# A gated linear attention feeding a mixture of four attention experts: three tile shapes on TensorE, and TensorE's order taken from a list scheduler in the source

## The chip, the core and the metric

One NeuronCore of one Trainium2 chip runs the whole program. The metric is device time in microseconds of one execution. A TensorE (PE) matmul names the part of the array that it uses: 128x128 (all of it), 64x128 (half of the rows), 128x64 or 128x32 (a half or a quarter of the columns). Matmuls on different parts of the array can run side by side.

## The reference

The first half is a gated linear attention over 4 batches, 8 heads, 768 steps, head size 48; its output is the input x of the second half, four causal attention experts of head size 64, of which each token takes two.

```python
for t in range(S):
    state = alpha[:, :, t, :, None] * state + np.einsum('bhd,bhe->bhde', k[:, :, t], v[:, :, t])
    y[:, :, t] = np.einsum('bhd,bhde->bhe', q[:, :, t], state)
...
logits = x @ w_gate                      # top 2 of 4, softmax over the two
for e in range(E):
    q = x @ wq[e]; k = x @ wk[e]; v = x @ wv[e]
    scores = scale * (q @ k.transpose(0, 2, 1))      # causal
    scores = scores - scores.max(-1, keepdims=True)
    a = np.exp(scores)
    a /= a.sum(-1, keepdims=True) + 1e-09
    ye = a @ v @ wo[e]
    out += mask[..., None] * w[:, :, kk:kk + 1] * ye
```

## The kernel before, in words

**The linear attention** goes in 24 chunks of 128 steps, 6 for each batch. For chunk n, `prep_r` and `prep_c` (L172, L185) make the decay products: two scans of 112x516 and one or two multiplies on VectorE (DVE), and from chunk 6 on one multiply on GpSimd (POOL). `gla_a` (L199) forms key times query for 8 heads in 64x128 tiles (`pa`); DVE masks one half into `ms`, ScalarE (ACT) copies and POOL masks the other. `gla_t` (L218) transposes the keys (`pt`, `kt`), `gla_u` (L228) updates the state with `pu`, in 128x64 tiles with 48 columns used, and `gla_y` (L252) makes the output `py` in 128x32 tiles, four abreast; ACT and DVE split it into `xh` and `xl`. `check` (L195) is one square on ACT that looks for lost precision.

**The experts** go in 8 units u of 384 tokens, three chunks each; two units make a batch, and an odd unit (hf = 1) sees twice the keys. `front(u)` has four projections `proj` (`pj`, 9 matmuls of 128x384 each), three value blocks `vproj` (`pv`, 9 of 128x260) and the gate. `back(u)` works on two pairs of experts: `top` (L471) finds each query's maximum over scores in 64x128 tiles (`sm`, reduced by DVE at L491 and L494), `toprow` transposes the three results (`pm`), and `score` (L507) forms the transposed scores (`sc`, 8 matmuls a step, two abreast; a step is one block of 128 keys), which ACT turns into exponentials `at` (L523), POOL masks on the diagonal (L525) and adds up into `as` (L533, L536). `av` (L538) multiplies them by the values (`yv`, two experts abreast in 128x64 tiles), and `sums` (L556) forms the denominators `ss` of one pair, two abreast in 128x32 tiles. `fin(u)` has `factor`, `scale` (transposes `pr`) and three `outp` (`po`, 6 matmuls of 128x384 each). There are 6 score steps in an even unit's back and 12 in an odd one's, 72 in all.

**Order.** PSUM has 8 banks, all under one tag. The head (chunks 0 to 2) and the body (unit 0's front, chunk 3's start) are in an order written by hand. From there Python generators are mixed: `mix` (L653) always advances the stream with the smallest cost divided by its weight, so `back(u)`, `front(u+1)` and the chunks of the half after next alternate with fixed weights (L44 to L52). What is emitted is then ordered on each engine by the framework's own scheduler. `AHEAD = 3` and `GROUP = 3` set how far `av` trails `score`. Loads are issued from ACT's queue in `gla` (L374), outputs from SyncE's (SP).

```python
b, g = back(0), half(1)
mix((b, MIX_BACK0), (g, MIX_GLA), until=g)
for u in range(NU - 2):
    mix((b, MIX_BACK[u]), (front(u + 1), MIX_FRONT[u]), (half(u + 2), 12.0))
    b = back(u + 1, fin(u))
```

Of the kernel before, what the change touches and what calls it, by code (L numbers as in the profile page):

```python
# [19 lines left out]
NE, HD = 4, 64  # L20
# [20 lines left out]
AHEAD = 3  # L41
GROUP = 3

HOP = 100  # L44
MIX_BACK0 = 6
MIX_BACK = (6, 22, 14, 22, 14, 22)
MIX_FRONT = (10, 10, 10, 10, 10, 10)
MIX_BACK6 = 10
MIX_TAIL6 = 20
MIX_TAIL7 = 28  # L50
MIX_FRONT7 = 12
MIX_GLA = 10  # L52
# [3 lines left out]
def tile_gla_moe(ctx: ExitStack, tc: tile.TileContext, qk_d, al_d, v_d, wqk_d, wv_d, wo_d, nat_d, vn_d, out_d):  # L56
# [142 lines left out]
    def gla_a(n):  # L199
        t = gl["qk", n]  # L200
        ms = work.tile([128, 2, 4, C], F32, name="ms", bufs=1)
# [16 lines left out]
    def gla_t(n):  # L218
# [5 lines left out]
        kt = gin.tile([128, 4, P], F32, name="kt")  # L224
# [3 lines left out]
    def gla_u(n):  # L228
# [50 lines left out]

    zb = d1r.rearrange("p a b -> p (a b)").bitcast(BF)[:, 0:256]  # L280
# [7 lines left out]
    cmask = consts.tile([128, 640], BF)  # L288
# [6 lines left out]
    def late_consts():  # L295
# [4 lines left out]
        A.activation(cmask[:, 512:640], sel, AF.Copy)  # L300
# [73 lines left out]
    def gla(h):  # L374
        for n in range(HALF * h, HALF * h + HALF):
            if n == HALF:
                prep_r(n + 1)
                yield
                prep_c(n + 1)
                yield  # L380
            if n + 2 < NG:
                load_v(n + 2, A)
            if n + 3 < NG:
                load_al(n + 3, 0, 4, A)
                load_q(n + 3, 0, 4, A)
            gla_y(n)
            gla_u(n)
            if n + 1 < NG:
                gla_a(n + 1)
                if (n + 1) % NC != NC - 1:  # L390
                    gla_t(n + 1)
            yield
            if n + 2 < NG:
                prep_r(n + 2)
                yield
                prep_c(n + 2)
                yield
                check(n + 1)
            yield


    mo = {}
    W3 = 384

    def proj(u, pair, which):
# [32 lines left out]
    def gate(u):  # L438
# [14 lines left out]
        w = work.tile([128, 3, NE], F32, name="gw")  # L453
# [17 lines left out]
    def top(u, pair, i):  # L471
        b, hf = divmod(u, 2)
        q, k = mo["q", u, pair], mo["k", b, pair]
# [4 lines left out]
        c1 = 384 if n == 640 else min(n, 512)  # L478
# [3 lines left out]
        for c0, c1 in pieces:  # L482
            w = c1 - c0
            pp = [gp("sm0"), gp("sm1")]
            for e in (0, 1):
                r = slice(64 * e, 64 * e + 64)
                mm(pp[e][:, :w], q[r, 0, 128 * i:128 * i + 128], k[r, 0, c0:c1], max(w, 256) / 4.8, start=True, stop=True,
                   tile_position=(64 * e, 0))
            for e in (0, 1):
                if c1 < n:  # L490
                    V.tensor_reduce(mp[:, e:e + 1], pp[e][:, :w], axis=AX.X, op=OP.max)  # L491
                else:
                    junk = work.tile([128, 512], BF, name="junk", bufs=2)
                    V.tensor_tensor_reduce(junk[:, :w], pp[e][:, :w], cmask[:, 640 - w:640], 1.0,  # L494
                                           -3.0e38 if c0 == 0 else mp[:, e:e + 1], OP.add, OP.max, mx[:, i, 64 * e:64 * e + 1])

    def toprow(u, pair):
# [5 lines left out]
        mr = work.tile([128, W3], F32R, name="mr", bufs=2)  # L503
# [3 lines left out]
    def score(u, pair, j):  # L507
        b, hf = divmod(u, 2)
        q, k, mr = mo["q", u, pair], mo["k", b, pair], mo["mr", u, pair]
# [4 lines left out]
        js = slice(128 * j, 128 * j + 128)  # L514
# [12 lines left out]
        if j == 1:  # L527
            s = work.tile([128, 2, W3], F32, name="as", bufs=2)
# [9 lines left out]
    def av(u, pair, j):  # L538
        b, hf = divmod(u, 2)
        at = mo.pop(("at", u, pair, j))  # L540
# [15 lines left out]
    def sums(u, pair):  # L556
        s = mo.pop(("as", u, pair))
        if pair == 0:
            mo["ss", u] = work.tile([128, W3], F32, name="ss", bufs=1)
        ss = mo["ss", u]  # L560
        ps_ = gp("ss")
        for e in (0, 1):
            r = 64 * pair + 32 * e
            mm(ps_[r:r + 32, :W3], ones32, s[:, e], W3 / 1.2, start=True, stop=True, tile_position=(0, r))
        r = slice(64 * pair, 64 * pair + 64)
        A.activation(ss[r], ps_[r, :W3], AF.Copy)
# [43 lines left out]

    def front(u):
# [10 lines left out]
    def fin(u):  # L622
        yield factor(u)
        for pair in (0, 1):
            yield scale(u, pair)
        for i in range(3):
            yield outp(u, i)

    def back(u, before=None):
        before = before or iter(())  # L630
        for pair in (0, 1):
            for i in range(3):
                yield top(u, pair, i)
            if pair == 0:
                yield next(before, None)
            yield toprow(u, pair)
        nj = 3 * (u % 2) + 3
        steps = [(pair, j) for pair in (0, 1) for j in range(nj)]
        for x in range(0, len(steps) + AHEAD, GROUP):
            for p, j in steps[x:x + GROUP]:  # L640
                yield score(u, p, j)
            yield next(before, None)
            for p, j in steps[max(0, x - AHEAD):max(0, x - AHEAD + GROUP)]:
                yield av(u, p, j)
                if j == nj - 1:
                    yield sums(u, p)
        yield from before

    def chain(*gs):
        for x in gs:  # L650
            yield from x

    def mix(*streams, until=None):  # L653
        live = [[g, w, 0.0] for g, w in streams if g is not None]
        while live and (until is None or any(x[0] is until for x in live)):
            x = min(live, key=lambda z: z[2] / z[1])
            c0 = cost[0]
# [158 lines left out]
```

## Time and profile before

| | |
|---|---|
| median of 3 runs | 434.1 us (432.31 to 435.65) |
| the profiled execution's own time | 432.75 us |
| its span, first to last instruction | 431.0 us |
| mean granted TensorE clock, share of 2.4 GHz | 0.924 |
| PE busy | 392.5 us, 91% |
| DVE, ACT, POOL busy | 255.9, 181.9, 183.8 us |

PE's busy time is made of modelled ends: a matmul counts from its start until its result is out, so matmuls in a stream overlap, and a short wait hides between two of them. What a matmul costs in a stream is therefore read from start to start. PEclk is the granted clock as a share of 2.4 GHz; 0.50 is 1.2 GHz.

### The profile page before, as it was taken

The numbers are of one execution on the slowest core, as the hardware profiler recorded it, in microseconds if no ns is written. First come the engines' busy times: TensorE is split into PE (matmuls) and PEld (weight loads), VectorE is DVE, ScalarE is ACT, GpSimd is POOL, SyncE is SP. The second block draws the span as 40 slices with busy tenths as digits, with TensorE's granted clock in tenths as the row PEclk, the third lists the DMA queues.
The fourth block names the chain that finished last, engine by engine and source line by source line (L and its number), as shares of the span: only waits on it lengthen the run. The fifth ranks groups of instructions, "written<-read, shape, count | busy, mean of one in ns | idle before, by whom it ended". The sixth has DMA issues, their size and how long they took to land.

```text
span 431.0 us, 9692 instructions
## 1 busy us (share of the span) xinstructions
PE 392.5 (91%) x3914; PEld 290.9 (67%) x3914; DVE 255.9 (59%) x615; ACT 181.9 (42%) x422; POOL 183.8 (43%) x234
## 2 busy tenths in 40 slices
PE   7989796998998799999998979999999999999953
PEld 5679475776676577777686756877677767646633
DVE  5979999899974537574955614472743324661120
ACT  1265352653263525534264344553244525335621
POOL 2122199543177560761249460370127433307520
PEclk9899776999699989999889969999979999999966
DMA  8936436454041422323222301201000010001101
GB/s 236 325 103 205 151 110 187 136 161 149 0 113 45 136 73 68 108 73 98 69 84 70 113 37 44 68 26 40 17 2 2 20 38 0 2 19 38 56 2 64
DMA packets 14022, 35.41 MB, mean 82 GB/s; under 512 B 1616, under 2 KB 5136, under 8 KB 13968
## 3 DMA queue, kind: packets, MB, share of 16 engines
q10 hardware_dynamic: 7600, 22.02, 16.8%
q1 hardware_dynamic: 6368, 12.68, 9.1%
q8 instruction: 33, 0.54, 0.6%
q14 instruction: 21, 0.17, 0.1%
HBM read 29.98 MB, written 4.72 MB: 80 GB/s over the span
## 4 chain that ended last, share of the span: by engine, by line
PE 53%; DVE 14%; POOL 9%; issue 8%; ACT 7%; DMA 6%; SPq 0%; ACTq 0%; POOLq 0%; DVEq 0%
PE pj L73 12%; PE sc L73 7%; PE yv L73 7%; PE po L73 7%; DMA al<-in_al_dram 5%; PE py L73 4%; PE pv L73 3%; DVE al L178 3%; PE sm L73 3%; PE pa L73 2%; PE ss L73 2%; ACT al L197 2%; POOL as L536 2%; DVE al L189 2%; POOL qk L183 2%
## 5 line engine op out<-in xcount | busy, mean ns | idle before, releaser
L536 POOL TENSOR_TENSOR as<-as,at 128x256 f32<-128x256 f32 (+2 forms) x40 | 56.2, 1404 | 13.9 <-DVE gmx L466 8.8
L523 ACT ACTIVATE at<-sc 128x384 f32<-128x384 f32 (+1 forms) x144 | 50.2, 425 | 12.4 <-PE sc L73 11.1
L73 PE MATMUL sc<-q,k 64*128 64x384 f32 (+2 forms) x432 | 53.1, 339 | 0.3 <-ACT at L523 0.3
L533 POOL TENSOR_TENSOR as<-at 128x512 f32<-128x512 f32 (+1 forms) x16 | 26.7, 1668 | 62.1 <-ACT at L523 61.5
L73 PE MATMUL yv<-at,vg 128*64 128x384 f32 (+2 forms) x288 | 46.5, 439 | 4.9 <-DVE xl L277 3.3
L178 DVE TENSOR_TENSOR_SCAN al<-al,d1r 112x516 f32<-112x516 f32 (+1 forms) x25 | 36.7, 1471 | 15.2 <-DMA al<-in_al_dram 15.2
L73 PEld LDWEIGHTS sc<-q,k 64*128 64x128 f32 x432 | 36.7, 191 | 13.3 <-issue 6.4
L250 POOL TENSOR_TENSOR S<-st,ev 48x192 f32<-48x192 f32 x32 | 20.6, 644 | 54.1 <-DVE st L249 53.1
L525 POOL TENSOR_SCALAR_AFFINE_SELECT at<-at 128x256 f32<-128x256 f32 x48 | 26.8, 558 | 35.4 <-ACT at L523 35.4
L73 PE MATMUL pj<-xh,wqk_h 128*128 128x384 f32 x96 | 38.8, 404 | 1.8 <-DVE xl L277 1.0
L494 DVE CUSTOM_DVE_ANT_0 junk<-sm,cmask 128x128 bf16<-128x128 f32 (+3 forms) x64 | 28.2, 481 | 19.1 <-PE sm L73 19.0
L73 PE MATMUL py<-ms,v 128*32 128x128 f32 x768 | 37.8, 287 | 1.2 <-DVE ms L212 0.9
L73 PE MATMUL sm<-k,q 64*128 64x256 f32 (+3 forms) x128 | 32.9, 431 | 5.1 <-DVE ms L212 1.6
L197 ACT ACTIVATE al<-al 112x1032 f32<-112x1032 f32 x23 | 24.5, 1065 | 28.4 <-POOL qk L183 22.6
L73 PE MATMUL pj<-xl,wqk_h 128*128 128x384 f32 x96 | 35.5, 370 | 0.1
L73 PE MATMUL pj<-xh,wqk_l 128*128 128x384 f32 x96 | 35.1, 366 | 0.0
L73 PEld LDWEIGHTS yv<-at,vg 128*64 128x64 f32 x288 | 18.0, 139 | 23.7 <-issue 13.3
L189 DVE TENSOR_TENSOR_SCAN al<-al,d1c 112x516 f32<-112x516 f32 (+1 forms) x25 | 33.5, 1343 | 0.6
L73 PE MATMUL pa<-qk 48*128 48x128 f32 x384 | 28.2, 285 | 2.6 <-DVE qk L193 2.1
L73 PEld LDWEIGHTS sm<-k,q 64*128 64x128 f32 x128 | 16.9, 201 | 20.3 <-issue 5.3
L181 POOL COPY ev<-al 112x4 f32<-112x4 f32 (+1 forms) x25 | 8.2, 330 | 51.5 <-DVE al L178 34.0
L73 PEld LDWEIGHTS py<-ms,v 128*32 128x32 f32 x768 | 24.3, 114 | 8.0 <-issue 2.8
(119 smaller groups left out, 835.0 us busy)
## 6 DMA issues: line engine op xcount, KB each, us to landing
al<-in_al_dram ACTq DMA_DIRECT2D x18, 451.5 KB, 3.6
qk<-in_qk_dram ACTq DMA_DIRECT2D x18, 448.0 KB, 4.1
v<-in_v_dram ACTq DMA_DIRECT2D x19, 256.0 KB, 3.7
out_dram<-ot SPq DMA_DIRECT2D x24, 192.0 KB, 1.8
al<-in_al_dram SPq DMA_DIRECT2D x5, 451.5 KB, 6.2
qk<-in_qk_dram SPq DMA_DIRECT2D x5, 448.0 KB, 7.6
v<-in_v_dram SPq DMA_DIRECT2D x5, 256.0 KB, 8.3
wqk<-in_wqk_dram SPq DMA_DIRECT2D x1, 768.0 KB, 12.9
```

The source lines that it names most:

```text
L73: return PE.matmul(out, lhsT, rhs, **kw)
L178: V.tensor_tensor_scan(r.rearrange("p a w -> p (a w)"), r.rearrange("p a w -> p (a w)"), d1r[0:P, sl].rearrange("p a w -> p (a w)"), 0.0, ...
L181: G.tensor_copy(gl["ev", n][0:P, sl], r[:, :, C])
L183: G.tensor_tensor(t[0:P, sl, C:2 * C], t[0:P, sl, C:2 * C], r[:, :, 0:C], OP.mult)
L189: V.tensor_tensor_scan(c.rearrange("p a w -> p (a w)"), c.rearrange("p a w -> p (a w)"), d1[0:P, sl].rearrange("p a w -> p (a w)"), 0.0, O ...
L197: A.activation(al, al, AF.Square, accum_out=acc[0:P, n:n + 1])
L250: G.tensor_tensor(Ln[rows, :, cols], st[rows], e, OP.mult)
L494: V.tensor_tensor_reduce(junk[:, :w], pp[e][:, :w], cmask[:, 640 - w:640], 1.0, -3.0e38 if c0 == 0 else mp[:, e:e + 1], OP.add, OP.max, mx ...
L523: A.activation(at[:, e, lo:W3], pp[e][:, :w], AF.Exp)
L525: G.affine_select(at[:, :, lo:lo + 128], at[:, :, lo:lo + 128], [[0, 2], [1, 128]], OP.is_ge, 0.0, base=0, channel_multiplier=-1)
L533: G.tensor_tensor(s[:, :, lo:W3], a0[:, :, lo:W3], at[:, :, lo:W3], OP.add)
L536: G.tensor_tensor(s[:, :, lo:W3], s[:, :, lo:W3], at[:, :, lo:W3], OP.add)
```

## The change

Three things change. **Tile shapes:** `av` splits each expert's 64 output columns into two tiles of 32, so that four 128x32 tiles run abreast instead of two 128x64; `gla_u` does the same (48 becomes 32 and 16); and `sums` is called once a unit for all four experts, four abreast. The 128x64 shape is gone. **Keys:** each unit's keys have a tile of their own (384 columns, three buffers for each pair), so `top` cuts at multiples of 384 instead of 512, and the raw weights of queries and keys come in two transfers. A few buffers grow (`ms` 1 to 2, `kt` 2 to 3, `mr` and `as` 2 to 3), `junk` shrinks. **Order:** the generators and weights are gone. Behind the body every PE job is in a list, with its tile shape, a PE time, the jobs it needs, the PSUM banks and buffers it takes, the work it causes on DVE, ACT and POOL, and a target time (a chunk every `PACE = 11` us). The loop in `run()` takes the job with the lowest start delay plus 0.04 of the distance to its target; a change of tile shape counts as 0.2 us. PE runs exactly this order; the other engines are still ordered by the framework.

```diff
-AHEAD = 3
-GROUP = 3
-MIX_BACK = (6, 22, 14, 22, 14, 22)
...
+PACE = 11.0
+PULL = 0.04
+SWITCH = 0.2
+PREP = 1.0
...  gla_u
-            for s in (0, 1):
-                mm(pu[64 * s:64 * s + D, p], kt[:, p, 64 * s:64 * s + D], v[:, p, 80 * s:80 * s + D], 62,
-                   start=True, stop=True, tile_position=(0, 64 * s))
+            for r in (0, 32, 64, 96):
+                w = 32 if r % 64 == 0 else 16
+                o = 80 * (r // 64)
+                mm(pu[r:r + w, p], kt[:, p, r:r + w], v[:, p, o:o + D], 25, start=True, stop=True, tile_position=(0, r))
...  top
-        c1 = 384 if n == 640 else min(n, 512)
+        c1 = min(n, W3)
...  av
-        for e in (0, 1):
-            eg = 2 * pair + e
-            mm(py[64 * e:64 * e + 64, lo:W3], v[:, j % 3, 64 * eg:64 * eg + 64], at[:, e, lo:W3],
-               (W3 - lo) / 1.2 + 26, start=(j == 0), stop=(j == nj - 1), tile_position=(0, 64 * e))
+        for r in (0, 32, 64, 96):
+            col = 128 * pair + r
+            mm(py[r:r + 32, lo:W3], v[:, j % 3, col:col + 32], at[:, r // 64, lo:W3], (W3 - lo) / 2.4 + 13,
+               start=(j == 0), stop=(j == nj - 1), tile_position=(0, r))
...  sums
-    def sums(u, pair):
+    def sums(u):
+        ps_ = gp("ss")
+        for pair in (0, 1):
+            t = mo.pop(("as", u, pair))
+            for e in (0, 1):
+                r = 64 * pair + 32 * e
+                mm(ps_[r:r + 32, :W3], ones32, t[:, e], W3 / 2.4, start=True, stop=True, tile_position=(0, r))
+        ss = work.tile([128, W3], F32, name="ss", bufs=1)
+        A.activation(ss, ps_[:, :W3], AF.Copy)
...  two of the jobs, and the loop
+            job(("a", n), 64, 0.95, lambda: gla_a(n), [("prep", n - 2)] if n > HALF + 1 else [], n - 1.0, 2, (("V", 0.6), ("A", 0.5), ("G", 0.62)),
+                take=("ms",))
+                job(("s", u, pair, j), 64, 4 * max(w, 256) / 2080.0, lambda p=pair, j=j: score(u, p, j),
+                    [("r", u, pair)] + ([("s", u, pair, j - 1)] if j else []), tt, 2, tuple(af),
+                    take=("at",) + (("as",) if j == 1 else ()), give=("mr", "q") if j == nj - 1 else ())
+                    ready = max(ready, now + (SWITCH if x["mode"] != mode else 0))
+                    v = ready - now + PULL * (x["target"] - now)
...
-    mix((b, MIX_BACK0), (g, MIX_GLA), until=g)
+    with tc.manual_schedule(engines={mybir.EngineType.PE}):
+        run()
```

The job of `prep(n)` counts 3.2 us on DVE and 1.05 on ACT, and none on POOL.

The order of instructions moves as follows. First place, PE, where unit 1's row maxima are found (`sm` scores, `pm` transposes of the maxima, `pr` transposes of unit 0's factors). Before:

```order
L573 MATMUL pr<-ident,ss 128x128 x3
L502 MATMUL pm<-ident,mx_126 128x128
L73 MATMUL sm_1460<-k_578,q 128x512
L502 MATMUL pm<-ident,mx_126 128x128
L73 MATMUL sm_1461<-k_578,q 128x512
L73 MATMUL sm_1469<-k_578,q 128x384
L73 MATMUL sm_1470<-k_578,q 128x384
L73 MATMUL sm_1475<-k_578,q 128x256
L502 MATMUL pm<-ident,mx_126 128x128
L73 MATMUL sm_1476<-k_578,q 128x256
L73 MATMUL sm_1484<-k_578,q 128x512
L73 MATMUL sm_1485<-k_578,q 128x512
```

After, at the last of that unit's row maxima (`sc` and `yv` are score steps and value products of the same unit's other pair, `pt` a chunk's key transposes):

```order
L65 MATMUL sc_1478<-mr,msel 128x384
L65 MATMUL sc_1479<-mr,msel 128x384
L65 MATMUL yv<-at,vg 32x384 x4
L65 MATMUL sm_1498<-k_604,q 128x384
L65 MATMUL sm_1499<-k_604,q 128x384
L65 MATMUL sm_1504<-k_1226,q 128x384
L65 MATMUL sm_1505<-k_1226,q 128x384
L216 MATMUL pt<-ident,qk 128x112 x4
L467 MATMUL pm<-ident,mx_126 128x128 x3
```

The three transposes stand together, and score steps stand between the groups of `sm`.

Second place, PE, at the denominators `ss`. Before, one pair of unit 1:

```order
L73 MATMUL yv<-at,vg 64x384 x2
L73 MATMUL yv<-at,vg 64x256 x2
L73 MATMUL yv<-at,vg 64x128 x2
L73 MATMUL ss<-as,ones_123 32x384 x2
L73 MATMUL sm_2003<-k_1514,q 128x128
```

After, unit 0, both pairs:

```order
L65 MATMUL pj<-xh,wqk_l 128x384
L65 MATMUL yv<-at,vg 32x128 x4
L65 MATMUL ss<-as,ones_125 32x384 x4
L65 MATMUL pv<-wv_h,xh 128x260
L65 MATMUL pv<-wv_l,xh 128x260
```

`yv` and `ss` now have one shape, and `ss` comes once a unit with four abreast.

Third place, POOL, between two of the masks that `gla_y` needs (`ms`), in batch 2 (`as` the running sums, `qk` and `ev` decay products, `S` the state). Before:

```order
L215 AFFINE_SELECT ms<-ms 128x512
L183 TENSOR_TENSOR qk<-qk,al 112x4x128
L533 TENSOR_TENSOR as<-at 128x768
L536 TENSOR_TENSOR as<-as,at 128x768
L525 AFFINE_SELECT at<-at 128x2x128
L536 TENSOR_TENSOR as<-as,at 128x768
L250 TENSOR_TENSOR S_92<-st,ev 48x4x48 x2
L181 COPY ev<-al 112x4
L215 AFFINE_SELECT ms<-ms 128x512
```

After:

```order
L174 COPY ev<-al 112x4 x2
L498 TENSOR_TENSOR as<-at 128x768
L501 TENSOR_TENSOR as<-as,at 128x768
L498 TENSOR_TENSOR as<-at 128x768
L490 AFFINE_SELECT at<-at 128x2x128
L501 TENSOR_TENSOR as<-as,at 128x768 x2
L490 AFFINE_SELECT at<-at 128x2x128
L176 TENSOR_TENSOR qk<-qk,al 112x4x128
L501 TENSOR_TENSOR as<-as,at 128x2x256
L244 TENSOR_TENSOR S_90<-st,ev 48x4x48 x2
L174 COPY ev<-al 112x4
L208 AFFINE_SELECT ms<-ms 128x512
```

More of the running sums stand in front of the mask.

## Rows read from the trace of the kernel before

**Rows 1.** The page: busy time of each engine, and DVE and the granted clock (PEclk) in 40 slices, in tenths.

```profile
PE 392.5 (91%) x3914; PEld 290.9 (67%) x3914; DVE 255.9 (59%) x615; ACT 181.9 (42%) x422; POOL 183.8 (43%) x234
...
DVE  5979999899974537574955614472743324661120
...
PEclk9899776999699989999889969999979999999966
```

**Rows 2.** Busy time in four stretches, us (x instructions) of PE, PEld (weight loads), DVE, ACT, POOL, then PEclk, DMA share, GB/s.

```profile
0.00:40.00 40.00, 34.31 (x391) 27.90 (x391) 31.50 (x53) 15.04 (x28) 10.12 (x37) 0.96 0.75 229
40.00:120.00 80.00, 71.29 (x833) 53.00 (x832) 76.41 (x162) 34.16 (x75) 38.99 (x48) 0.85 0.40 123
120.00:400.00 280.00, 266.79 (x2583) 196.11 (x2583) 144.59 (x393) 122.79 (x298) 126.13 (x142) 0.96 0.17 54
400.00:431.00 31.00, 20.07 (x110) 13.90 (x109) 3.40 (x9) 9.87 (x23) 8.60 (x8) 0.77 0.12 42
```

**Rows 3.** PE in order of time, 285 to 295 us: start, duration, line, matmul, tile, moving operand, count.

```profile
285.26 0.29 PE L73 MATMUL pv<-wv_l,xh 128*128 128x260 f32 x1
285.39 0.28 PE L73 MATMUL pv<-wv_h,xl 128*128 128x260 f32 x1
285.60 0.43 PE L73 MATMUL py<-ms,v 128*32 128x128 f32 x8
...
287.28 0.56 PE L73 MATMUL pu<-v,kt 128*48 128x48 f32 x16
287.77 1.16 PE L73 MATMUL pa<-qk 48*128 48x128 f32 x16
...
290.20 0.84 PE L73 MATMUL ss<-as,ones 128*32 128x384 f32 x4
290.97 0.44 PE L73 MATMUL po<-wo_h,yh 128*128 128x384 f32 x1
...
293.34 0.34 PE L73 MATMUL pj<-xl,wqk_h 128*128 128x384 f32 x1
293.52 0.33 PE L73 MATMUL pj<-xh,wqk_l 128*128 128x384 f32 x1
293.78 1.52 PE L73 MATMUL yv<-at,vg 128*64 128x384 f32 x12
```

**Rows 4.** Weight loads (PEld) grouped by form: count, then busy us, mean ns of one, idle before.

```profile
L73 PEld LDWEIGHTS py<-ms,v 128*32 128x32 f32 x768 | 24.3, 114 | 8.0 <-issue 2.8 <-DVE ms L212 2.8 <-ACT at L523 1.0
L73 PEld LDWEIGHTS yv<-at,vg 128*64 128x64 f32 x288 | 18.0, 139 | 23.7 <-issue 13.3 <-DVE xl L277 3.4 <-POOL at L525 2.3
L73 PEld LDWEIGHTS pu<-v,kt 128*48 128x48 f32 x320 | 9.0, 127 | 4.3 <-issue 3.7 <-ACT q L423 0.2 <-ACT at L523 0.2
```

**Rows 5.** The start of chunk 10's output on PE, in order of time.

```profile
121.40 0.43 PE L73 MATMUL py<-ms,v 128*32 128x128 f32 x8
```

**Rows 6.** Some of DVE's groups by form over the whole span: count, busy us, mean ns, idle before.

```profile
L189 DVE TENSOR_TENSOR_SCAN al<-al,d1c 112x516 f32<-112x516 f32 x23 | 32.1, 1399 | 0.6
...
L212 DVE TENSOR_TENSOR ms<-pa,mask 128x512 f32<-128x512 f32 x27 | 18.3, 687 | 1.6 <-PE pa L73 1.0
...
L424 DVE TENSOR_TENSOR k<-pj,k 128x384 fp32r<-128x384 f32 x16 | 8.8, 548 | 19.7 <-ACT k L423 19.7
L494 DVE CUSTOM_DVE_ANT_0 junk<-sm,cmask 128x384 bf16<-128x384 f32 x16 | 8.2, 552 | 0.0
L491 DVE TENSOR_REDUCE mp<-sm 128x1 f32<-128x384 f32 x16 | 8.1, 548 | 0.0
L494 DVE DVE_READ_ACCUMULATOR2_ANT mx<- 128x1 f32 x96 | 7.9, 82 | 0.0
```

**Rows 7.** PE in order of time where unit 5's row maxima are found, 306 to 314 us.

```profile
306.05 1.16 PE L73 MATMUL sm<-k,q 64*128 64x384 f32 x8
...
309.61 0.78 PE L73 MATMUL sm<-k,q 64*128 64x384 f32 x2 [0.16 <-DVE mp L491]
310.41 0.33 PE L502 MATMUL pm<-ident,mx 128*128 128x128 f32 x1
310.67 1.70 PE L73 MATMUL sm<-k,q 64*128 64x256 f32 x5
...
312.80 0.69 PE L73 MATMUL pj<-xh,wqk_h 128*128 128x384 f32 x1
313.29 0.53 PE L73 MATMUL pj<-xl,wqk_h 128*128 128x384 f32 x1
313.61 0.53 PE L73 MATMUL pj<-xh,wqk_l 128*128 128x384 f32 x1
```

**Rows 8.** Busy time around the row maxima of units 3 and 5, columns as in rows 2.

```profile
203.00:213.00 10.00, 9.46 (x104) 5.98 (x96) 9.94 (x30) 2.40 (x6) 2.96 (x5) 0.96 0.27 81
213.00:220.00 7.00, 7.00 (x31) 5.48 (x31) 4.52 (x14) 2.31 (x6) 0.00 (x0) 0.57 0.00 0
...
311.00:318.00 7.00, 6.85 (x25) 5.08 (x23) 5.12 (x19) 1.72 (x4) 0.00 (x0) 0.51 0.02 4
```

**Rows 9.** The end, in order of time.

```profile
412.40 0.84 PE L73 MATMUL ss<-as,ones 128*32 128x384 f32 x4 [0.37 <-POOL as L536]
```

**Rows 10.** Two of POOL's groups by form: count, busy us, mean ns, idle before.

```profile
L536 POOL TENSOR_TENSOR as<-as,at 128x768 f32<-128x768 f32 x16 | 29.9, 1868 | 11.9 <-DVE gmx L466 8.8 <-ACT at L523 2.2
...
L183 POOL TENSOR_TENSOR qk<-qk,al 112x512 f32<-112x512 f32 x18 | 24.9, 1383 | 5.7 <-DMA qk<-in_qk_dram 4.8 <-PE pm L502 0.9
```

More of the change, by code (lines that the diff above doesn't have):

```diff
@@ L200, in gla_a @@
         t = gl["qk", n]
-        ms = work.tile([128, 2, 4, C], F32, name="ms", bufs=1)
+        ms = work.tile([128, 2, 4, C], F32, name="ms", bufs=2)
         gl["ms", n] = ms
@@ L527, in score @@
         if j == 1:
[L528 removed]
+            s = work.tile([128, 2, W3], F32, name="as", bufs=3)
             mo["as", u, pair] = s
@@ L554, in av @@
             mo["y", u, pair] = y
-    def sums(u, pair):
[L557 to L560, printed above, removed]
-        ps_ = gp("ss")
[L562 to L566, printed above, removed]
+    def sums(u):
+        ps_ = gp("ss")
+        for pair in (0, 1):
[5 more added lines that the diff above has]
+        A.activation(ss, ps_[:, :W3], AF.Copy)
+        mo["ss", u] = ss
     def factor(u):
@@ L609, in outp, with gates @@
         SY.dma_start(out_d[b, t0:t0 + 128, :], ot)
+    def gates(u):
+        for _ in gate(u):
+            pass
     def front(u):
@@ L620, in front @@
                 yield from gate(u)
-    def fin(u):
-        yield factor(u)
-        for pair in (0, 1):
-            yield scale(u, pair)
-        for i in range(3):
[L627 to L657, printed above, removed]
-            if next(x[0], 1) == 1:
-                live.remove(x)
-            x[2] += cost[0] - c0 + HOP
-    half = lambda h: gla(h) if h < NU else None
+    def tops(u, pair):
+        return [(lambda i=i: top(u, pair, i)) for i in range(3)]
@@ new lines, in scores, with prep, job @@
+    def scores(u, pair, j0=0, j1=None):
+        return [(u, pair, j) for j in range(j0, 3 * (u % 2) + 3 if j1 is None else j1)]
+    def prep(n):
+        if n == HALF:
+            prep_r(n + 1)
+            prep_c(n + 1)
+        if n + 2 < NG:
+            load_v(n + 2, A)
+        if n + 3 < NG:
+            load_al(n + 3, 0, 4, A)
+            load_q(n + 3, 0, 4, A)
+        if n + 2 < NG:
+            prep_r(n + 2)
+            prep_c(n + 2)
+            check(n + 1)
+    jobs = []
+    def job(key, mode, pe, fn, deps, target, banks=0, after=(), take=(), give=()):
+        jobs.append(dict(key=key, mode=mode, pe=pe, fn=fn, deps=deps, target=target * PACE, banks=banks, after=after,
+                         take=take, give=give))
@@ L742, in tile_gla_moe @@
                 V.tensor_tensor(xl[:, :, ts], p3, xh[:, :, ts].bitcast(F32), OP.subtract)
-            for _ in chain(front(u), back(u), fin(u)):
+            for _ in front(u):
                 pass
+            for pair in (0, 1):
+                for f in tops(u, pair):
+                    f()
+                toprow(u, pair)
+                for x in scores(u, pair):
+                    score(*x)
+                    av(*x)
+            sums(u)
+            factor(u)
+            for pair in (0, 1):
+                scale(u, pair)
+            for i in range(3):
+                outp(u, i)
 def _pack(q, k, v, alpha, w_gate, wq, wk, wv, wo):
```

265 lines of the change are left out of this document (175 added, 90 removed).

## The prediction

> **What bounds the kernel now.** I began with the busy shares and the slices over time [rows 1]. PE is busy for 392.5 of 431.0 us, while DVE is at 9 tenths in most slices of the first third and at half or less behind it. So I cut the span in four by the windows view [rows 2]. From 40 to 120 us DVE works 76.4 of 80 us, 95%, and PE has 8.7 us idle and a clock of 0.85: DVE bounds this stretch. From 120 to 400 us DVE works 144.6 of 280 us and PE 266.8: PE bounds it, with 13.2 us idle and, at a clock of 0.96, 11.2 us of full-speed time withheld (0.04 x 280). Behind 400 us a chain of single steps bounds. Then I read PE in order of time, from start to start [rows 3], since its busy time hides both changes of tile shape and short waits. Two matmuls of 384 columns in one shape start 0.18 us apart (293.34, 293.52); the next, in another shape, 0.26 later. From one value block matmul to the next it is 0.13, into `py` 0.21. A change of tile shape so costs 0.09 us.
>
> **The change part by part**, against the profiled execution's span of 431.0 us.
>
> *Tile shapes changed less often.* Counted in the instruction order up to the final test, neighbours on PE with different shapes fall from 331 to 191. 140 x 0.09 is 12.6 us off. All of it is on PE; where PE waits anyhow a change hides in the wait, so this is an upper end (in the DVE-bound stretch some is lost, and I count that below).
>
> *Sums.* Now 16 calls, each 0.77 us from start to the next group, 0.68 without the change of shape [rows 3]. Eight remain, with four tiles side by side for the same columns: 8 x 0.68 = 5.4 us off.
>
> *Value products.* As many columns go through: two matmuls two abreast become four four abreast. `py`, already four abreast, runs at its columns' pace, so I count 0. *State updates.* 16 matmuls in 0.49 us, 0.40 without the change of shape [rows 3], become 32. By columns, eight rounds of 48 as now, nothing is added (somewhat less than nothing, -1 us, where the four fill up a round better). By weight loads there is another end: 768 loads of 32 columns occupy 24.3 us, 0.032 each [rows 4]; if nothing hid them, 576 + 640 loads after, against 18.0 + 9.0 us for both groups now, add 38.9 - 27.0 = 12 us. I take +4 for both together: the loads of `py` hide behind 128 columns, which 48 columns can do only in part. The ends are -1 and +12.
>
> A rule bears on the state updates. TensorEngine Tiling (Array Packing) in the Trainium skill, section Performance Considerations, gives each matmul about 60 cycles of overhead, says one of a single column takes as long as one of 60, and advises against taking a tile factor from a dimension that is small already. By it, as an estimate, 320 more matmuls of 60 cycles at 2.4 GHz would add 8 us; the sum would end 4 us higher than mine. The row that bears on it is 16 matmuls in 0.40 us, 25 ns each, which a limit by columns gives as well.
>
> *Row maxima.* The cut at 384 adds a matmul pair and two short reductions where 512 keys went in one piece: 8 pairs, some 0.06 us each, +0.5 on PE. DVE gets some 3 us more, beside PE.
>
> *The DVE-bound stretch.* Chunk 10's output starts at 121.4 us now [rows 5]. Counting instructions ahead of it in both orders: score steps go from 10 to 18, value products from 6 to 17, projections from 10 to 12, value blocks from 6 to 9, output matmuls from 0 to 18. At four strides of 0.175 (0.70), 0.6 (by the `yv` rows, some are narrow), nine strides of 0.175 (1.57), nine of 0.12 (1.1) and one of 0.17 us [rows 3] that is 5.6 + 6.6 + 3.1 + 3.3 + 3.1 = some 21 us of PE work that now lies behind 120 us. DVE pays for it in the same stretch: one more second scan (1.40), one more mask (0.69), two splits (0.55 each), a gate, a scaling and six pieces of row maxima, together 11 us by rows like these [rows 6]. If DVE stays the bound, chunk 10 comes 11 us later and takes 21 us of PE work with it: 10 us off. It is less if PE then stalls there itself (0), and at most the whole idle and withheld time, 8.7 + 0.15 x 80 = 20.7.
>
> *Row maxima of odd units.* From 306.05 to 312.80 us [rows 7] PE issues 18 `sm` matmuls, three `pr` and a few `pm`: nine pairs of some 0.16, seven transposes at 0.11 and a dozen changes at 0.09 make 3.4 us, the stretch takes 6.75. PE waits for DVE's reductions with nothing else in its order. Right behind, the clock falls: matmuls of 384 columns start 0.32 apart, which is 1.2 GHz, and it is 0.51 over 7 us. So unit 5 costs 3.4 us of waits and 0.49 x 7 = 3.4 of clock. Unit 3's clock falls in the same place, 0.43 x 7 = 3.0 [rows 8], and I put its waits at unit 5's 3.4. For unit 7, where the clock holds, I take 2 us. In the new order score steps and a chunk's work stand between the groups of `sm`, and the transposes stand together, behind the last. DVE's work remains, but PE has something to do: -15 us if all is covered. Both ends: 0 if PE's fixed order waits as long elsewhere, and -24 (13.2 idle and 11.2 withheld, everything visible between 120 and 400 us).
>
> *The end.* The last running sum releases `ss` [rows 9]. In the new order unit 7's twelve score steps have less other work beside them, so POOL's sums (1.87 us each at full width [rows 10]) bound them rather than PE; but the whole begins sooner. I count 0, with ends -4 and +4.
>
> *Buffers, two transfers for the weights, one ACT copy for the sums instead of two:* 0. The ACT copy lies beside PE's next job, the transfers beside chunks 1 and 2 (PE is busy for 34.3 of the first 40 us [rows 2]); were they late, the first projection would wait, for which 1 us is in the range.
>
> The sum: 431.0 - 12.6 - 5.4 + 4 + 0.5 - 10 - 15 = 392.5 us of span. With the 1.75 us around it (432.75 - 431.0) that is 394. The median of the runs shown is 1.3 us above the profiled execution, less than the spread of the three runs.
>
> **The rivals.**
>
> *The waits come back elsewhere.* PE's order is now fixed by rough job costs, and a cover that is early by one job is worth nothing. For it: the job list counts nothing on POOL for `prep`, where `qk` alone takes 1.38 us [rows 10], and counts a row maximum of 384 keys as 0.93 us on DVE, where two reductions of some 0.63 are needed [rows 6]. Against it: behind 120 us DVE and POOL are busy for only half the time, so a job delayed by 1 us has room to catch up. Then only the PE work counts: 431 - 12.6 - 5.4 + 4.5 = 417.5, or 419 with its surroundings.
>
> *POOL's queue decides, and it gets slower.* The place is `gla_y`, which waits for the POOL mask of `ms`; in the new order PE has some 2 us of work (a score step, transposes, a value product) between `gla_a` and `gla_y`. POOL takes instructions in order, and before the mask in the second batch stand five full-width sums where three stood. Two of them and a `qk`, 2 x 1.87 + 1.38, are 5.1 us, 3 more than the cover. At 3 us on each of 18 chunks (6 to 23, beside which score steps run) the time is 394 + 54 = 448. It decides from 2.5 us a chunk. Against it: POOL is busy 126 of 280 us, and `gla_a` may now run ahead, since `ms` has two buffers.
>
> *Weight loads run alone.* If the loads of four tiles with the same rows did not overlap with matmuls, 576 x 0.114 + 640 x 0.114 instead of 288 x 0.139 + 320 x 0.127 us would add 58 us where I count 4: 394 + 54 = 448. Against it: 768 loads of 0.114 us are 88 us, and the rows have them in 24.3 [rows 4]; that excludes all but a part. TensorE: Matmul & The Clock Gate in the Trainium skill, Part 3, states that weight loads overlap with running matmuls only where their row groups differ; `py`'s four tiles share all rows, and by that rule the trace does not agree.
>
> **How the numbers follow.** My forecast, with its own range of 374 to 410: 0.67. The waits come back, 408 to 425: 0.21. POOL's queue: 0.10. Loads alone: 0.02. The range of 366 to 424 leaves out the two slow cases and the tails of the first, some 0.18. A change of 1% is about what a measurement of this kernel can tell. Faster by more than that takes nearly all of the first two: 0.83; within 1%, the edge of the second and of the third: 0.05; slower, 0.12.
>
> **What would show it.** Right: changes of shape down by 140 and still 0.09 each; no `sm` stretch of 6 us with interleaved `pm`; a clock above 0.95 from 120 us on; chunk 10's output near 132 us; eight groups of `ss` of the old length. Wrong: `pu` over 0.7 us a chunk; `py` matmuls that wait for POOL's masks; PE idle behind 120 us over 25 us; chunk 10 past 140 us, which would put the DVE-bound stretch wrong.

## The result, and the profile after

The changed kernel takes 420.8 us (median of 4 runs, 419.95 to 422.30) against 434.7 us; the ratio is 0.9692, 95% interval 0.9642 to 0.9743: 3.1% faster. The forecast was 394 us, 9.2% under the 434.1 us on record. The profiled execution took 419.95 us with a span of 418.2. The time is near that of my first rival, "the waits come back elsewhere", which gave 419; whether for its reason is asked below. All ratios below are to the kernel before on the same chip, 0.01 is 4.3 us. They are of means and leave disturbed executions out, so that one can differ from the quotient of the medians.

The page after, busy time and two lines of the 40 slices (to be held against [rows 1]):

```profile
PE 363.4 (87%) x4538; PEld 287.5 (69%) x4538; DVE 251.5 (60%) x631; ACT 182.1 (44%) x414; POOL 182.5 (44%) x234
...
DVE  4879999777845275463987565366842364473020
...
PEclk9799779898989898979989999999999999989958
```

The same four stretches as [rows 2], with the same columns:

```profile
0.00:40.00 40.00, 33.35 (x431) 27.69 (x432) 30.11 (x51) 14.95 (x28) 8.74 (x36) 0.91 0.75 222
40.00:120.00 80.00, 64.64 (x800) 52.14 (x802) 67.37 (x156) 34.54 (x78) 33.75 (x40) 0.87 0.36 110
120.00:400.00 280.00, 257.47 (x3284) 201.43 (x3276) 151.13 (x418) 128.72 (x304) 140.00 (x159) 0.96 0.19 61
400.00:418.00 18.00, 7.93 (x31) 6.23 (x29) 2.89 (x8) 3.85 (x7) 0.00 (x0) 0.69 0.12 39
```

PE is busy for 29 us less, but the span is only 12.8 us shorter. PE's idle time grew from 8.7 to 15.4 us between 40 and 120 us, and from 13.2 to 22.5 between 120 and 400; the clock of that long stretch is 0.96 as before. DVE, which was to stay the bound at 95%, is busy for 67.4 of 80 us.

PE in order of time after, at two places (start, duration, line, matmul, tile, moving operand, count), against [rows 3]:

```profile
252.61 0.64 PE L65 MATMUL yv<-at,vg 128*32 128x256 f32 x8
253.07 0.83 PE L65 MATMUL ss<-as,ones 128*32 128x384 f32 x8
253.72 0.40 PE L65 MATMUL yv<-at,vg 128*32 128x128 f32 x8
...
298.03 0.54 PE L65 MATMUL pu<-v,kt 128*32 128x48 f32 x32 [0.23 <-DVE xl L271]
298.50 0.60 PE L216 MATMUL pt<-ident,qk 112*128 112x112 f32 x4
```

Eight matmuls of sums, four side by side, take 0.65 us from start to start, where a call for half of them took 0.68 without its change of shape. 32 state updates take 0.47 us with a change of shape behind them, where 16 took 0.49. The weight loads say the same (groups by form, as in [rows 4]):

```profile
L65 PEld LDWEIGHTS yv<-at,vg 128*32 128x32 f32 x576 | 13.6, 110 | 30.0 <-POOL at L490 20.7 <-issue 5.4 <-ACT at L488 0.6
L65 PEld LDWEIGHTS pu<-v,kt 128*32 128x32 f32 x320 | 11.4, 119 | 3.8 <-issue 2.6 <-DVE mx L459 0.3 <-DVE qk L186 0.3
```

Twice as many loads for the value products occupy 13.6 us instead of 18.0.

Chunk 10's output starts 35 us later than in [rows 5], and 24 us later than I said:

```profile
156.22 0.41 PE L65 MATMUL py<-ms,v 128*32 128x128 f32 x8
```

Both kernels pass this point, so the span can be split there. Ahead of it and behind it, columns as in [rows 2], first before, then after:

```profile
0.00:121.40 121.40, 107.01 (x1235) 81.87 (x1235) 108.72 (x215) 50.60 (x108) 49.27 (x85) 0.89 0.51 157
121.40:431.02 309.62, 285.45 (x2682) 209.05 (x2680) 147.19 (x400) 131.26 (x316) 134.58 (x150) 0.94 0.17 53
...
0.00:156.22 156.22, 129.18 (x1649) 105.05 (x1653) 116.45 (x252) 63.88 (x139) 67.40 (x101) 0.90 0.43 129
156.22:418.22 262.00, 234.21 (x2893) 182.45 (x2885) 135.05 (x379) 118.17 (x276) 115.08 (x133) 0.94 0.18 59
```

Ahead of chunk 10's output PE is busy for 22.2 us more, near the 21 us of work that I had counted as moved there, and idle for 27.0 us instead of 14.4. Behind it the changed kernel takes 262.0 us. The prediction had 132.4 us ahead (121.4 + 11) and so 260.1 behind (392.5 - 132.4). Of the 25.7 us by which the span was missed, 23.8 lie ahead of this point and 1.9 behind it.

Where unit 5's second pair finds its row maxima, the stretch of [rows 7] is gone; score steps, a value product and a chunk's work stand between, and the three transposes together:

```profile
302.23 0.34 PE L65 MATMUL sm<-k,q 64*128 64x384 f32 x1
303.05 1.36 PE L65 MATMUL sm<-k,q 64*128 64x384 f32 x3 [0.49 <-DVE ms L205]
303.99 1.18 PE L65 MATMUL sc<-q,k 64*128 64x384 f32 x6
...
309.27 0.55 PE L467 MATMUL pm<-ident,mx 128*128 128x128 f32 x3
```

What came in its place is in PE's waits (total us, times, longest us). The first line is from before, when the value products waited 1.2 us in all for POOL's masks, the others from after:

```profile
PE yv L73 <- POOL at L525: 1.2, 2, 1.1
...
PE yv L65 <- POOL at L490: 16.1, 11, 5.0
PE pm L467 <- DVE mx L459: 7.4, 9, 2.2
```

Of the 16.1 us, 4.6 lie ahead of chunk 10's output and 11.5 behind. Ahead of it most of the longest waits are for DVE:

```profile
PE pm L467 <- DVE mx L459: 5.3, 5, 2.2
PE yv L65 <- POOL at L490: 4.6, 2, 2.5
PE sm L65 <- DVE q L389: 3.9, 1, 3.9
PE pa L65 <- DVE qk L186: 3.6, 3, 1.5
```

The longest wait for a mask, first in POOL's order of time and then in PE's:

```profile
172.80 0.41 POOL L490 TENSOR_SCALAR_AFFINE_SELECT at<-at 128x256 f32<-128x256 f32 x1
173.29 0.72 POOL L501 TENSOR_TENSOR as<-as,at 128x256 f32<-128x256 f32 x1
175.79 2.57 POOL L176 TENSOR_TENSOR qk<-qk,al 112x512 f32<-112x512 f32 x1 [1.78 <-issue]
178.32 1.33 POOL L490 TENSOR_SCALAR_AFFINE_SELECT at<-at 128x256 f32<-128x256 f32 x1
```

```profile
172.71 0.34 PE L65 MATMUL pj<-xl,wqk_h 128*128 128x384 f32 x1
172.88 0.33 PE L65 MATMUL pj<-xh,wqk_l 128*128 128x384 f32 x1
173.15 1.16 PE L65 MATMUL pa<-qk 48*128 48x128 f32 x16
174.24 0.43 PE L65 MATMUL yv<-at,vg 128*32 128x128 f32 x8
179.71 1.51 PE L65 MATMUL yv<-at,vg 128*32 128x384 f32 x8 [5.04 <-POOL at L490]
```

A mask of 0.4 to 1.3 us stands in POOL's queue behind a later chunk's `qk`, whose transfer was issued only at 169.52, took 6.2 us to land, and which takes 2.6 us itself; the mask starts as `qk` ends. PE has a value product next and stands still for 5 us. In this stop the clock falls, and it stays low behind it, as with the row maxima of [rows 8]:

```profile
176.00:184.00 8.00, 4.29 (x22) 2.83 (x23) 7.90 (x11) 0.66 (x2) 5.42 (x6) 0.57 0.17 54
```

### The profile page after: what moved, and what is told of

Read it like the earlier page. It is cut to its first block, busy times and chain, and to the rows that moved or that the text cites. A ratio compares the mean times of both kernels' runs of the same rounds, so it can differ in the third digit from the quotient of the medians.

```text
span 418.2 us, 10900 instructions
## 1 busy us (share of the span) xinstructions
PE 363.4 (87%) x4538; PEld 287.5 (69%) x4538; DVE 251.5 (60%) x631; ACT 182.1 (44%) x414; POOL 182.5 (44%) x234
## 4 chain that ended last, share of the span: by engine, by line
PE 58%; DVE 14%; POOL 13%; issue 6%; DMA 5%; ACT 2%; DVEq 0%; POOLq 0%; ACTq 0%
PE pj L65 9%; PE py L65 8%; PE sc L65 8%; PE po L65 8%; PE yv L65 7%; PE pv L65 6%; POOL as L501 5%; DMA qk<-in_qk_dram 4%; DVE junk L459 3%; PE pa L65 3%; POOL qk L176 3%; PE sm L65 3%; POOL at L490 2%; PE ss L65 2%; DVE qk L186 1%
## 5 line engine op out<-in xcount | busy, mean ns | idle before, releaser
L488 ACT ACTIVATE at<-sc 128x384 f32<-128x384 f32 (+2 forms) x144 | 51.3, 420 | 39.5 <-PE sc L65 35.8
L65 PE MATMUL yv<-at,vg 128*32 128x384 f32 (+2 forms) x576 | 51.0, 435 | 16.1 <-POOL at L490 16.1
L65 PEld LDWEIGHTS sc<-q,k 64*128 64x128 f32 x432 | 35.6, 191 | 18.6 <-issue 10.7
L171 DVE TENSOR_TENSOR_SCAN al<-al,d1r 112x516 f32<-112x516 f32 (+1 forms) x25 | 32.0, 1282 | 17.0 <-DMA al<-in_al_dram 15.6
L208 POOL TENSOR_SCALAR_AFFINE_SELECT ms<-ms 128x512 f32<-128x512 f32 x21 | 15.3, 728 | 51.4 <-ACT ms L207 51.2
L498 POOL TENSOR_TENSOR as<-at 128x512 f32<-128x512 f32 (+1 forms) x16 | 27.0, 1686 | 22.2 <-ACT at L488 21.7
L65 PE MATMUL pj<-xh,wqk_h 128*128 128x384 f32 x96 | 34.9, 363 | 1.9 <-DVE xl L271 1.3
L176 POOL TENSOR_TENSOR qk<-qk,al 112x512 f32<-112x512 f32 x18 | 27.7, 1537 | 18.7 <-DMA qk<-in_qk_dram 11.9
L65 PEld LDWEIGHTS yv<-at,vg 128*32 128x32 f32 x576 | 13.6, 110 | 30.0 <-POOL at L490 20.7
L271 DVE TENSOR_TENSOR xl<-py,xh 128x384 fp32r<-128x384 f32 x24 | 13.3, 553 | 31.6 <-ACT xh L270 31.6
L190 ACT ACTIVATE al<-al 112x1032 f32<-112x1032 f32 x23 | 24.5, 1063 | 17.5 <-POOL qk L176 10.7
L65 PEld LDWEIGHTS pa<-qk 48*128 48x128 f32 x384 | 26.4, 201 | 8.2 <-DVE qk L186 4.6
L456 DVE TENSOR_REDUCE mp<-sm 128x1 f32<-128x384 f32 x48 | 25.4, 552 | 9.9 <-PE sm L65 9.7
```

The lines of the kernel that those rows point to most:

```text
L65: return PE.matmul(out, lhsT, rhs, **kw)
L171: V.tensor_tensor_scan(r.rearrange("p a w -> p (a w)"), r.rearrange("p a w -> p (a w)"), d1r[0:P, sl].rearrange("p a w -> p (a w)"), 0.0, ...
L176: G.tensor_tensor(t[0:P, sl, C:2 * C], t[0:P, sl, C:2 * C], r[:, :, 0:C], OP.mult)
L190: A.activation(al, al, AF.Square, accum_out=acc[0:P, n:n + 1])
L208: G.affine_select(ms[:, s], ms[:, s], [[0, 4], [1, C]], OP.is_ge, 0.0, base=-(C - 1), channel_multiplier=1)
L271: V.tensor_tensor(xl[:, :, 128 * g:128 * g + 128], py, xh[:, :, 128 * g:128 * g + 128].bitcast(F32), OP.subtract)
```

## The experiments

"us" is the median; the last column is the difference to the changed kernel by the ratios.

| run | edit | us | ratio to before (95%) | to the changed kernel |
|---|---|---|---|---|
| e1 | before, new shapes, old mix | 427.9 | 0.988 (0.980 to 0.996) | +7.9 |
| e2 | after, old shapes, same order | 422.3 | 0.971 (0.961 to 0.981) | +0.7 |
| e8 | after, change of shape priced 0 | 421.1 | 0.975 (0.968 to 0.982) | +2.7 |
| e12 | before, short row maxima | 415.8 | 0.962 (0.956 to 0.967) | |
| e13 | before, more PE work in the start | 437.0 | 1.014 (1.008 to 1.020) | |
| e10 | after, chunks earlier | 433.1 | 1.000 (0.995 to 1.005) | +13.3 |
| e11 | after, short row maxima | 408.6 | 0.942 (0.936 to 0.948) | -11.7 |
| e3 | after, costs of the job list mended | 428.1 | 0.982 (0.972 to 0.992) | +5.5 |
| e9 | after, pace 14 | 435.1 | 1.006 (1.001 to 1.011) | +15.9 |
| e6 | after, PE's order free | 418.1 | 0.969 (0.965 to 0.974) | 0 |
| e4 | after, `qk` on DVE | 420.2 | 0.969 (0.962 to 0.977) | 0 |
| e14 | after, `ms` off DVE | 419.1 | 0.972 (0.964 to 0.980) | +1.1 |
| e5 | after, no diagonal masks | 409.7 | 0.949 (0.944 to 0.954) | -8.9 |
| e18 | before, no diagonal masks | 428.9 | 0.990 (0.984 to 0.995) | |
| e16 | e5 and e11 | 401.2 | 0.926 (0.921 to 0.930) | -18.9 |
| e17 | e6 and e14 | 416.1 | 0.954 (0.947 to 0.960) | -6.7 |
| e19 | e4 and e14 | 414.4 | 0.961 (0.957 to 0.964) | -3.8 |
| e20 | e4, e6 and e14 | 412.2 | 0.953 (0.948 to 0.958) | -7.0 |

**What the shapes are worth.** e1 puts the new `av`, `gla_u` and `sums` into the kernel before; e2 puts the old `av` and `gla_u` into the kernel after; e8 sets one number.

```
 e8  -SWITCH = 0.2
     +SWITCH = 0.0
```

> The kernel before with only the new shapes: value products and state updates in four tiles side by side, one sums group per unit, the old mix of streams. Changes of shape in the instruction order fall only from 331 to 308, because the old mix sets other shapes between. Theory A (what came of the gain is shapes and sums, a change costs 0.09 us, more loads cost nothing): 23 x 0.09 + 8 x 0.68 = 7.5 us off, 431.0 to 423.5 us of span, about 425 us in all. Rival (the waits come back whatever is changed): 430 to 434. Rival (more weight loads cost): above 434.

> The changed kernel with the value products and state updates two tiles abreast as before; the order is the same job by job. Changes of shape rise from 191 to 229. Theory A: 38 x 0.09 = 3.4 us on, about 424 us. Rival (the loads of four tiles cost what the shapes give): at or under 420 us. Rival (more waits, since a value product's columns are no longer shared): above 428.

> The changed kernel with the scheduler's price of a change of shape set to 0 instead of 0.2: the order has 264 changes of shape instead of 191, everything else as in the changed kernel. Theory A (a change costs 0.09 us of PE, waits do not depend on the grouping): 73 x 0.09 = 6.6 us more, about 427 us. Rival (grouping by shape is paid with waits for operands): waits fall by as much, 418 to 422.

e1 gains 5.4 us (1.9 to 8.8) where 7.5 were expected: that fits sums and 23 fewer changes at their cost in the trace, with loads that cost little, but does not price them one by one. e2 points the same way but, at +0.7 us with some 4 either way, settles nothing. e8 has 73 more changes, so by the rows 6.6 us more PE work, and its time lies between 1 us below the changed kernel's and 6 above. Its trace shows where some of it went:

```profile
PE pm L467 <- DVE mx L459: 9.4, 6, 5.3
PE yv L65 <- POOL at L490: 6.5, 8, 2.2
```

Without the price for a change, PE waits 9.6 us less for masks and 2.0 more for row maxima. Whether grouping by shape pays in net is not settled.

**What bounds the first stretch.** e12 takes DVE work away from it, e13 gives PE work to it, e10 moves chunks ahead in it.

```
 e12 -V.tensor_reduce(mp[:, e:e + 1], pp[e][:, :w], ...)
     +V.tensor_reduce(mp[:, e:e + 1], pp[e][:, :128], ...)     (junk's reduction likewise)
 e13  gla_y(n)
     +if 4 <= n <= 10:
     +    warm(12)
 e10  t = target * PACE
     +if key[0] in ("a", "t", "y", "u", "prep"):
     +    t = HALF * PACE + (target - HALF) * 8 - max(0, target - 12) * -4.0
```

> The kernel before with row maxima over the first 128 columns of each piece only (part of the reduction is left out). If the row maxima of the odd units cost it 15 us of waits and clock, as predicted: about half of that and the first third's DVE work off, 416 to 422. Rival (those waits lie beside others): 428 to 432.

> The kernel before with 12 extra matmuls of 256 columns (some 1.3 us, results unused) behind gla_y of chunks 4 to 10: six of the seven lie ahead of chunk 10's output, with their changes of shape some 8.4 us of PE work in the stretch from 40 to 122 us, no work on DVE. If DVE bounds this stretch, as predicted: chunk 10's output at most 2 us later than 121.4, the time 0 to 3 us longer. Rival (PE's own row bounds it, and DVE's 95% are beside the point): chunk 10's output 8 us later or more, the time 8 to 11 us longer.

> The changed kernel with the chunks' targets 8 us apart up to chunk 12 (then 12 us) instead of 11: chunk 7 stands ahead of most of unit 1's projections and unit 0's output matmuls. Theory C (the order put 27 us of PE work between the outputs of chunks 6 and 7, DVE ran dry, and that is where the gain of the first 160 us went): chunk 10's output at about 130 us instead of 159, DVE busy 75 us between 40 and 120 instead of 67, the time 8 to 10 us shorter, about 411. Rival (the waits move elsewhere): 418 to 423 with chunk 10 as early.

Between 40 and 120 us e12 has 9.8 us less DVE work than [rows 2], and chunk 10's output starts where it started:

```profile
40.00:120.00 80.00, 70.09 (x833) 52.08 (x832) 66.60 (x162) 34.64 (x76) 37.56 (x48) 0.87 0.42 123
```

```profile
121.38 0.43 PE L73 MATMUL py<-ms,v 128*32 128x128 f32 x8
```

e13 has no more DVE work and some 8.4 us more PE work ahead of chunk 10's output, and this starts 9.8 us later:

```profile
131.20 0.43 PE L73 MATMUL py<-ms,v 128*32 128x128 f32 x8
```

So DVE's 95% did not bound this stretch: with 9.8 us less of its work the end moved by 0.02 us. PE's own row did, at its low clock and with its short waits. One rival is left: e13 puts its matmuls between `gla_y` and `gla_u`, in the chain of steps from chunk to chunk, and a bound by that chain would show the same. By the end e13 is 6 us slower: some is absorbed by later waits. e10 then has its chunks early (chunk 10's output at 125.80), and is 13 us slower: my theory that the late chunks were the loss fell. Its early chunk 10 has 8 score steps and 8 value products ahead of it where the changed kernel has 18 and 17; that work now lies behind.

```profile
40.00:120.00 80.00, 63.06 (x961) 53.18 (x959) 70.12 (x149) 34.76 (x77) 37.46 (x47) 0.88 0.46 135
120.00:160.00 40.00, 35.52 (x447) 28.34 (x447) 29.72 (x67) 15.69 (x36) 24.02 (x23) 0.85 0.28 84
160.00:400.00 240.00, 220.05 (x2600) 169.23 (x2600) 124.44 (x359) 108.53 (x257) 97.80 (x121) 0.96 0.16 49
```

PE idles 16.9, 4.5 and 20.0 us in these stretches and 14.3 behind 400 us; in the changed kernel it is 15.4, 5.0, 17.5 and 10.3. Why this order ends later I did not find.

**Is it the list's costs, or the fixed order?**

```
 e3  -("prep") (("V", 3.2), ("A", 1.05))          -("m") (("V", n / 500.0 + 0.16),)
     +(("V", 3.3), ("G", 1.9), ("A", 1.05))       +(("V", 0.42 + 0.0022 * n + (0.1 if n > W3 else 0)),)
 e9  -PACE = 11.0                                 +PACE = 14.0
 e6  -with tc.manual_schedule(engines={mybir.EngineType.PE}):
     -    run()
     +run()
```

> The changed kernel with two costs in its job list set to what the trace has: prep gets 1.9 us on POOL (none before), a row maximum 0.42 + 0.0022 n us on DVE (before 0.16 + 0.002 n), 0.1 more over 384 keys. Changes of shape 199. Theory B (PE waits because the list believes POOL and DVE to be free earlier than they are): PE's waits for the diagonal mask (16.1 us) and for row maxima (7.4) fall by half, idle time between 120 and 400 us from 22.5 to about 12, the time to about 409 us. Rival (any fixed order that is late against DVE's start waits as long): 418 to 424 with waits moved to other lines.

> The changed kernel with the scheduler's pace at 14 us a chunk instead of 11, near what the chip shows (24 chunks in some 335 us): other targets, another order, 200 changes of shape. If an order that is true to the chip's pace has fewer waits: under 414. Rival (any order of this list waits as long, in other places): 418 to 428.

> The changed kernel with PE's order not fixed: the framework orders PE's jobs as it did before, from the list in program order; changes of shape 197 instead of 191. Theory (waits come back because PE's order is fixed): waits for POOL's mask and for row maxima fall, 410 to 414. Rival (the order of the list sets the waits, fixed or not): 418 to 424.

Truer costs made another order and not a better one: at 428.1 us e3 is above both of its expectations. Its waits for masks halve, and others come:

```profile
PE yv L65 <- POOL at L490: 7.9, 8, 2.0
PE pv L65 <- DVE k L389: 5.3, 2, 2.7
PE sm L65 <- DVE q L389: 3.9, 1, 3.9
PE sm L65 <- DVE mp L456: 3.8, 3, 1.6
PE sc L65 <- DVE xl L271: 3.7, 2, 1.8
```

A pace near that of the chip (e9) is 16 us worse. Freed from its fixed order (e6), PE waits for masks as before, 17.0 us, and the ratio is the same. The order of the list sets the waits; over four lists (e3, e8, e9, e10) the time lies 3 to 16 us above this one. These runs suggest that its pace of 11 is a luckier order and not a truer model; why each list is as good as it is was not found.

**Row maxima and masks.** e11 is e12's edit in the changed kernel; e5 and e18 leave the `affine_select` of `score` out, e16 does both.

> The changed kernel with row maxima taken over the first 128 columns of each piece only (part of the reduction is left out): DVE's work for them falls from some 70 to some 43 us, PE's work and order unchanged. If the new order covers row maxima, as predicted: within 3 us of the changed kernel. Rival (they still set PE's waits): 8 to 15 us less, 406 to 412, with pm's waits (7.4 us) and sm's gone.

> The changed kernel without the diagonal masks of the scores on POOL (48 selects of some 0.41 us are left out); PE's order unchanged. Theory E (the cover won at the row maxima is lost again at POOL's masks, whose in-order queue holds them behind sums and qk): PE's waits for at fall from 16 us to under 6 and the time by 8 us or more, to 412 or less. Rival (these waits lie beside row maxima and exponentials): 417 to 421.

> The kernel before without the diagonal masks of the scores on POOL (the same 48 selects are left out). By theory E masks cost nothing in the old order: within 3 us of the kernel before. Rival (POOL's masks cost the same in both orders): 6 us less or more.

> The changed kernel without the diagonal masks and with row maxima over the first 128 columns of each piece (both are left out in part). Short maxima alone saved 12 us. If masks and maxima are waits in a row: both savings add, under 402. Rival (the one lies beside the other): 405 to 409.

Short row maxima save 16.5 us before and 11.7 after. By ACT's copies of the chunks' outputs, the one at 204.24 us before comes 0.5 us earlier and the next, at 223.97, 5.9 us: all the gain lies behind 200 us. After, chunk 10's copy (159.25) comes 5.2 us earlier, 1.1 of it an earlier start of the whole, the last copy 8.0 and the end 10.0; less than 5 us lie behind 160. e11's expectation asked for 3 us or less if the new order covers the maxima, and the time came out at the rival's 406 to 412: over the whole they are not covered. Behind 160 us, by these two traces, the greater part is. Masks are the other way: leaving them out saves 4.5 us before, between the two expectations of e18, and 8.9 after. The difference, 4.4 us with some 4 either way, is what the new order adds to their price. The 4.5 us came where PE's visible waits for masks were only 1.2, so the price is not those waits alone. e5's trace has no wait of `yv` for POOL left; its longest are 6.8 us in all for row maxima.

e16 saves 18.9 us of 8.9 + 11.7: the two stand in a row rather than one beside the other.

**Work taken off POOL's queue.**

```
 e4  -DVE_K = 6                                   +DVE_K = 24
 e14 -if s == 0 or n < HALF:                      +if n < HALF:                     (in gla_a)
```

> The changed kernel with the multiply of qk on DVE for all chunks (18 x 1.54 us off POOL, 18 x 0.7 us on DVE), PE's order unchanged. Theory B: POOL's mask comes when the scores are there, PE's waits for it fall from 16.1 us to under 6, the time to about 412 us. Rival (DVE bounds the first 160 us and takes 12.6 us more): chunk 10's output later than 159 us and the time 422 to 428. Rival (the waits for POOL lie beside others that end as late): 418 to 422.

> The changed kernel with both halves of ms copied by ACT and masked by POOL, as one half is already: 21 multiplies of 0.69 us off DVE (14.5 us), 21 x 0.60 on ACT, 21 x 0.63 on POOL; PE's order unchanged. If DVE's work still sets PE's waits for row maxima, at the rate of the shortened row maxima (12 us for 27 us of DVE work): 6 us less, 413 to 416. Rival (POOL's queue then holds up gla_y or the diagonal masks): 423 to 432.

> The changed kernel with PE's order left to the framework and both halves of ms masked by POOL, the two variants that measured 418 and 419 us. If their small gains are real and add: 415 to 417. Rival (each is no more than the spread of the runs): 418 to 421.

> The changed kernel with two exchanges: qk's multiply on DVE for all chunks (18 x 1.54 us off POOL, 18 x 0.7 on DVE) and both halves of ms copied by ACT and masked by POOL (21 x 0.69 off DVE, 21 x 0.63 on POOL): DVE's work stays within 2 us, POOL's falls by 14.5 us, ACT's grows by 12.6. Theory E (what stands in POOL's queue sets the waits): waits for the masks under 8 us without more waits for row maxima, 411 to 414. Rival (any exchange moves the waits): 418 to 421.

> As the run beside it, with PE's order left to the framework. Theory E: 409 to 413. Rival (any exchange moves the waits): 416 to 421.

e4 took 9.4 us of waits for masks away, and waits for DVE grew, at the same time (the trace is of its slowest execution, 424.8 us):

```profile
PE pm L467 <- DVE mx L459: 11.6, 11, 4.8
PE yv L65 <- POOL at L490: 6.7, 8, 2.5
PE pa L65 <- DVE qk L186: 5.0, 3, 2.5
PE pj L65 <- DVE xl L271: 4.2, 2, 3.7
```

e14 alone is no gain. e19, both edits, is faster than either kernel, at 414.4 us just beyond the 414 expected, and with no overlap of its interval with the changed kernel's. But its waits are not those that theory E asked for:

```profile
PE pm L467 <- DVE mx L459: 11.6, 11, 4.8
PE yv L65 <- POOL at L490: 9.2, 10, 2.5
```

Masks fell by 6.9 us, row maxima rose by 4.2. e20, with PE's order free, has the lowest ratio of those that compute the whole result, 412.2 us (407.3 to 414.4); its interval does not tell it from e17, whose six runs scatter from 409.6 to 423.2.

## Why the prediction was wrong

- **Changes of shape (-12.6).** 140 fewer, as counted. The price in the rows held: 0.17 us from matmul to matmul in one shape and 0.27 into another (172.71, 172.88, 173.15). No run tests it as time by itself: e1 has 23 of the changes, and e8, with 73 more, does not settle it.
- **Sums (-5.4), updates and value products (+4).** 0.65 us a call: held. The +4 was 0 or less by the rows. By the rule of the Trainium skill (TensorEngine Tiling (Array Packing), Performance Considerations), about 60 cycles of overhead for each matmul, one would take, as an estimate at 2.4 GHz, 25 ns. As a cost of each matmul in a stream that isn't borne out by 32 matmuls in 0.47 us, change of shape included, which is under 15 ns each.
- **The DVE-bound stretch (-10): this step failed.** I read a bound from a busy share of 95%, and forecast that chunk 10 would come 11 us later and take 21 us of PE work with it. e12 shows that the load on DVE did not set chunk 10's time, and e13 that PE work there costs its full length. So the work moved ahead of chunk 10 cost 22.2 us of busy PE time, nothing of it fell into waits, and PE's idle time rose by 12.6 us besides. Together that is the 34.8 us by which chunk 10 is late: instead of 10 us off, 14 us on. This is nearly the whole miss. The prediction named "chunk 10 past 140" as the sign of it. The longest of the waits there are for DVE's `mx`, `q` and `qk`, and for POOL's masks; why this order waits more for them was not isolated.
- **Row maxima of odd units (-15): right in its mechanism, and in part lost again.** The stretches with interleaved transposes are gone, and shorter maxima gain far less behind 160 us than before. But PE's next job now is more often a value product that needs a POOL mask, and I put no price on that. Those waits went from 1.2 to 16.1 us, the masks' price from 4.5 to 8.9 us, and the clock fell with the longest as it had with the maxima. In sum the terms behind chunk 10 held all the same, 262.0 us where 260.1 followed from the prediction. With the masks' waits paid there, other terms must have given more than I put: the loads that cost nothing are one. How the gain divides among them no run tells.
- **The end (0)** held: from the last sums to the end 18.6 us before, some 20 after.

**The first rival** came within 2 us, and waits did come back: PE's idle time rose from 38.6 to 54.8 us over the whole span. But 12.6 of these 16.2 us lie ahead of chunk 10, and its sum kept +4 for loads and updates that were not paid, so its number is in part luck. It named `qk`, uncounted on POOL, and I gave it 0.21 because POOL is half idle: half idle on average is no room in a queue served in order, where one late `qk` held a mask of 0.4 to 1.3 us for five. Yet neither counting `qk` (e3) nor taking it off POOL (e4) made the kernel faster, so it is seen in the longest wait and not shown to be the cause of the time.

The other rivals: POOL's queue did hold PE, but at the value products and not at `gla_y`, and for far less than the 54 us of that rival; loads alone did not happen.

## What to carry to other kernels

A share of 95% is not a bound until taking work off that engine moves the end of the stretch: a run with less work there and one with more on the other engine tell. Split a miss at a point that both kernels pass before looking for its cause. When a new order covers one wait, list what the covering jobs themselves wait for, above all short operations in a queue served in order that also holds work on late transfers. Count a removed stall as gain only once the next wait is priced.

## What the runs showed of the hardware

Four tiles of 32 columns side by side took 576 weight loads in 13.6 us where 288 of 64 columns took 18.0, though all four share their rows: such loads cost next to nothing here (their mean is 110 ns, 63 us one after another). One and the same select on POOL (128x256) took 0.41 us at 172.80 and 1.33 at 178.32, and one and the same multiply of `qk` 1.63 at 171.22 and 2.57 at 175.79; what slowed them was not tried.
